# Attention's tails moved behind the second outputs, and batch 2's transposes gathered into two runs

## The chip, the cores and the metric

The kernel runs on one core of one Trainium2 chip. The metric is the device time of one execution in microseconds; the median of three runs before the change is 314.04 us (313.4 to 314.63). PE is the matrix engine TensorE, ACT is ScalarE, DVE is VectorE, POOL is GpSimd, SP is SyncE, whose queue only issues DMAs.

## What is computed

The reference runs a causal attention with a decay, whose result is the input of a two-layer perceptron (cut to what matters):

```python
batch, n_heads, seq, head_dim = (8, 8, 576, 64)
scores = scale * np.matmul(q, k.transpose(0, 1, 3, 2))
cum = np.cumsum(np.maximum(s, 0.0), axis=-1)
bias = -(cum[:, :, :, None] - cum[:, :, None, :])
scores = np.where(causal, -1000000000.0, scores + np.minimum(bias, 0.0))
attn = softmax(scores)
x = matmul(attn, v).transpose(0, 2, 1, 3).reshape(B * S, H * D)    # 4608 x 512
h = x @ w_in                                                       # 512 x 2048
g = 0.5 * h * (1.0 + erf(h * inv_sqrt2))
return g @ w_out                                                   # 2048 x 512
```

## The kernel before

**Tiling.** The eight batches of attention give 8 x 576 = 4608 tokens, which the perceptron takes as nine chunks of 512. Chunk c needs the tokens of batches up to c alone, so batch c + 1 is computed inside chunk c. The work has no scheduler: each engine runs its instructions in the order in which the code issues them, so a line that is moved moves in every queue that it issues to.

**Attention of one batch.** q and k are transposed (for batches 0 to 2 on PE, `tr_mm`, L395, in 64 x 64 tiles, 36 matmuls for one of q and k of four heads; later by DMA). `sc_mm` (L434) makes scores, ACT takes their exponentials into `P` (L440), DVE masks them (`mask`, L448 and L453). `av_mm` (L463) multiplies by the values with tiles of 128 rows by 32 columns, four side by side: the denominators `av_d` (weights from `wb`) and the outputs `av_o` (weights from `vv`), for the first 512 rows of two halves of the heads (qd 0 and 1). `av_out` takes the reciprocals on ACT (L478, L479) and writes the product into `xT` on DVE (L503). The last 64 rows of a batch are its **tails**: `av_tails` runs 48 small matmuls into `av_t` (`tails_pe`), two ACT instructions and one DVE product, L524 (`tails_out`). Batch b's tails are first needed by chunk b + 1.

**The perceptron.** `l1_item(c, f2)` is one **pair**: two of the 16 columns of first-layer tiles, 4 + 4 matmuls of 128x512 into one pair of PSUM banks (`h_ps`, L550), and one Gelu on ACT (L558; the last pair's in two halves, L561). The second layer of chunk 0 runs in `l2_item` (L576). From chunk 1 on it is seven products of halves in place of eight (`prod`, L764, 16 matmuls of 128x256 each, results `o_al`, `o_be`, `o_ga`), between which the next batch's scores and outputs stand.

**Banks.** PSUM is held as five slots: x, y and z of two banks each, `M[0]` and `M[1]` of one each. `order[c]` says in which order chunk c uses x, y and z; pair f2 takes the slot f2 modulo 3. A slot is free once its last reader has finished.

**Around the change.** In chunks 0 and 1 the first two pairs are issued as their first two k-tiles, then the tails of batch c (into `M[0]`), then the other two k-tiles (L910 to L914). In chunks 1 to 6 the tails of batch c + 1 stand between product 4 and product 3 (L1046), into the slot y that the batch's first outputs used. In chunk 1, batch 2's four transposes (q and k of two halves) follow pairs 2, 3, 4 and 5 one by one, each into `M[0]` and `M[1]` with two DVE copies (L404). Behind pair 2 ACT runs `squares_v(1)` (L237, two instructions over the values of batch 1, for a check), after which POOL loads the k of batch 3 into the same buffer; behind pair 5 it runs `squares_v(2)`.

Of the kernel before, what the change touches and what calls it, by code (L numbers as in the profile page):

```python
# [19 lines left out]
def kernel(  # L20
# [10 lines left out]
    nc = tc.nc  # L31
# [195 lines left out]
    def absmax(b, p):  # L227

        nc.vector.tensor_reduce(  # L229
            amx[:, b * NP + p], qkT[b % 2][:, :, p, :S], axis=AX, op=ALU.max, apply_absolute_value=True  # L230
        )
# [174 lines left out]
    def tr_two(b, qd, i, engs):  # L406
        t_ps = [bank(m, [128, FR, 64], bf16, "tr_ps") for m in M]
        tr_mm(b, qd, i, t_ps)
        for pp in range(2):
            copy(  # L410
                engs[pp],
                qkT[b % 2][:, i, 2 * qd + pp, :S].rearrange("d (t r) -> d t r", r=FR),
                t_ps[pp].rearrange("d r t -> d t r"),
            )
# [73 lines left out]
    def av_pe(b, qd, den, two):  # L488

        oo = bank(two, [128, 2, 512], fp32, "av_o")  # L490
        o = [oo[:, t] for t in range(2)]
        av_mm(b, qd, den, None, MAIN)
        for t in range(2):
            av_mm(b, qd, o[t], t, MAIN)
        return o
# [12 lines left out]
    def av_main(b, qd, one, two):  # L508
        den = bank(one, [128, 512], fp32, "av_d")
        o = av_pe(b, qd, den, two)  # L510
        av_out(b, qd, den, o)
# [18 lines left out]
    def av_tails(b, slot):  # L530
        tails_out(b, tails_pe(b, slot))
# [364 lines left out]
    mask(0, 3, nc.vector)  # L896
    av_main(0, 0, M[0], Y)
    av_main(0, 1, M[1], Z)

    for c in range(NCH):  # L900
        nb = c + 1
        if nb >= B:
            l1_seven(c)
            if c < B:
                order[c + 1] = order[c]
            sums_a(c, (1, 2), HF // 2, HF)
            l2_seven(c)
            continue
        if c < 2:
            l1_item(c, 0, 0, KO - 2)  # L910
            l1_item(c, 1, 0, KO - 2)
            av_tails(c, M[0])
            l1_item(c, 0, KO - 2)
            l1_item(c, 1, KO - 2)  # L914
        else:
            l1_item(c, 0, 0, KO - 2)
            l1_item(c, 0, KO - 2)
            l1_item(c, 1)
        if 1 < c:
            transpose_tiles(nb)  # L920
            if nb + 1 < B:
                behind_g(qkT[nb % 2][0:1, 1, NP - 1, S - 1 : S])
                for n in "qk":
                    load_qk(nb + 1, n)
        for p in range(NP) if c == 0 else (0, 1) if c == 1 else (0, 1, 2):
            absmax(c, p)
        for f2 in range(2, FT // 2):
            l1_item(c, f2)
            if c == 1 and 2 <= f2 < 6:
                tr_two(2, f2 // 2 - 1, f2 % 2, both)  # L930
            if c == 1 and f2 == 2:
                squares_v(1)
                load_qk(3, "k")
            if c == 1 and 3 <= f2 < 5:
                scale_v(2, STS[f2 - 3 : f2 - 2], nc.vector)
            if c == 1 and f2 == 5:
                sums_a(c, (1, 2, 3), 0, HF // 2)
                scale_v(2, STS[2:4], nc.vector)
                squares_v(2)
            if c > 1 and f2 == 3:  # L940
                scale_v(nb, [(0, 4), (4, 5)], nc.vector)
                sums_a(c, (1, 2, 3), 0, HF // 2)
                absmax(c, 3)
                if c == B - 2:
                    sums_u((1, 2))
                    absmax(nb, 0)
            if c > 1 and f2 == 4:
                squares_v(nb)
                if nb + 1 < B:
                    behind(2, raws[nb + 1, "k"][0:1, ST - 2, 0, :])  # L950
                    load_v(nb + 1, [nc.sync])
        if c == 0:
            squares_v(0)
            sums_b((1, 2, 3, 4), 0, 4)
            exp_set()
            x, y, z = order[0]
            l2_item(c, 0, 0, 8)
            l2_item(c, 1, 0, 8)
            tr_one(1, 0, 0, nc.vector, z)
            tr_one(1, 0, 1, nc.scalar, x)  # L960
            l2_item(c, 2, 0, 8, y)
            sc_mm(1, 0, (z, x))
            l2_item(c, 3, 0, 8, y)
            sc_mm(1, 1, (z, x))
            mask(1, 0, nc.vector)
            sums_b((1, 2, 3), 4, 8)
            behind(1, w_out_r[0:1, FT - 5, 0:D])
            load_v(1, [nc.sync])
            l2_item(c, 0, 8, 12)
            l2_item(c, 1, 8, 12)  # L970
            tr_one(1, 1, 0, nc.vector, z)
            tr_one(1, 1, 1, nc.scalar, x)
            mask(1, 1, nc.vector)
            sums_b((4,), 4, 8)
            behind_v(1, 1)
            for qd in range(2):
                for n in "qk":
                    load_front(2, n, qd)
            l2_item(c, 2, 8, 12)
            l2_item(c, 3, 8, 12)  # L980
            sc_mm(1, 2, (z, x))
            l2_item(c, 0, 12, eng=nc.scalar)
            sc_mm(1, 3, (z, x))
            mask(1, 2, nc.vector)
            scale_v(1, STS, nc.vector)
            l2_item(c, 1, 12, eng=nc.scalar)
            l2_item(c, 2, 12, eng=nc.scalar)
            mask(1, 3, nc.vector)
            av_main(1, 0, M[0], z)
            l2_item(c, 3, 12)  # L990
            av_main(1, 1, M[1], x)
            order[1] = (y, z, x)
            load_v(2, [nc.sync])
            load_qk(3, "q")
        else:
            exp_set()
            sums_a(c, (1, 2), HF // 2, HF)

            x, y, z = order[c]
            order[nb] = (z, x, y)  # L1000
            add = nc.vector.tensor_tensor
            al_t = bank(M[0], [128, 2, 256], fp32, "o_al")
            al = [al_t[:, u] for u in range(2)]
            kept = [keep_sb(i, n) for i, n in enumerate(("q0", "k0", "q1"))]
            oa = [two_sb() for _ in range(2)]

            prod(c, 1, al, start=True)
            sc_mm(nb, 0, (z, x))
            sc_mm(nb, 2, (y,))
            copy(nc.vector, kept[0], al_t)  # L1010
            if c == 1:
                scale_v(2, STS[4:5], nc.vector)
                load_v(3, [nc.sync])
            be = bank(M[1], [128, 2, 256], fp32, "o_be")
            prod(c, 2, [be[:, u] for u in range(2)], start=True)
            prod(c, 6, al, 0, 6)
            mask(nb, 0, nc.vector)
            add(oa[0][:, :, N1], be, kept[0], op=ALU.add)
            sc_mm(nb, 2, (z,), 1)
            sc_mm(nb, 1, (x, y))  # L1020
            mask(nb, 2, nc.vector)
            prod(c, 6, al, 6)
            copy(nc.vector, kept[1], al_t)
            mask(nb, 1, nc.vector)
            sc_mm(nb, 3, (z, x))
            sums_a(c, (3, 4), HF // 2, HF)
            sums_a(c, (4,), 0, HF // 2)
            ga_t = bank(M[1], [128, 2, 256], fp32, "o_ga")
            ga = [ga_t[:, u] for u in range(2)]
            prod(c, 5, ga, start=True)  # L1030
            mask(nb, 3, nc.vector)
            if nb + 1 < B:
                behind_g(P_of[nb, 3][0:1, 1, PW - 1 : PW])
                cast_qk(nb + 1)
            den = bank(z, [128, 2, 512], fp32, "av_d")
            o = av_pe(nb, 0, den[:, 0], y)
            av_out(nb, 0, den[:, 0], o)
            prod(c, 7, al)
            copy(nc.scalar, kept[2], al_t)
            o = av_pe(nb, 1, den[:, 1], x)  # L1040
            add(oa[1][:, :, N2], ga_t, kept[2], op=ALU.add)
            av_out(nb, 1, den[:, 1], o)
            prod(c, 4, al)
            if c == B - 2:
                sums_x(c + 1, nc.vector)
            av_tails(nb, y)  # L1046
            copy(nc.scalar, oa[1][:, :, N1], al_t)
            if c == B - 2:
                nc.scalar.preload_act_table_set("gelu_and_others")
            store(c, 2, oa[1])  # L1050
            prod(c, 3, ga)
            add(oa[0][:, :, N2], ga_t, kept[1], op=ALU.add)
            store(c, 1, oa[0])
            if c == 1:
                absmax(1, 2)
                absmax(1, 3)
                square(7)
            elif nb < B - 1:
                square(c + 1 if c > 2 else 0)
            if c == 2:  # L1060
                cert_decay()
            if c == B - 2:
                sums_u((3,))
# [158 lines left out]
```

## Time and profile before

| | us |
|---|---|
| median of three runs | 314.04 |
| profiled execution | 314.03 |
| its span, first to last instruction | 312.2 |
| PE busy | 293.0 |
| ACT busy | 246.7 |
| DVE busy | 228.4 |
| POOL busy | 98.8 |

Times within the execution count from the span's start. In the timeline a row is a run of like instructions: start, length, engine, line, operation, output and inputs, shape, count, and in square brackets the idle time of the engine ahead of it with what ended it. Matmuls overlap in the array and their ends are modelled, so a row's length runs past the next row's start; the difference of two starts is the time that a run holds PE's queue. In the rows `128*128`, `128*32` and `64*64` are the tile of the array that a matmul uses. The chain of work lists what led to the last instruction, back from the end, in order of time.

### The profile page before, as it was taken

The page shows a single profiled execution, that of the slowest core. Times are in us where ns is not written, and L with a number is a line of the kernel's source. Part 1 is how long each engine was busy: PE and PEld are TensorE (multiplying, and loading weights), DVE is VectorE, ACT ScalarE, POOL GpSimd, SP SyncE. Part 2 cuts the span into 40 slices and gives each one's busy share as a digit, 9 for nine tenths or more (in the row PEclk, how much of TensorE's full clock was granted, in tenths as well). Part 3 has the DMA queues.
Part 4 walks back from the last instruction along what each step waited for, and adds up shares of the span by engine and source line. Part 5 has one row for each costly group of instructions (what it writes and reads, how often), then busy time and mean ns, then how long its engine had stood idle before and what let it go on. Part 6 is the DMA issues. An engine that isn't in the chain of part 4 may idle for free.

```text
span 312.2 us, 8460 instructions
## 1 busy us (share of the span) xinstructions
PE 293.0 (94%) x3522; PEld 194.8 (62%) x3522; DVE 228.4 (73%) x430; ACT 246.7 (79%) x348; POOL 98.8 (32%) x180
## 2 busy tenths in 40 slices
PE   0689999999999999999999999999999999999991
PEld 0564444545784578547854786477647887887780
DVE  3597337788879777696876597748798889856770
ACT  3687687798968996989788988798879877967830
POOL 6585007104070376228530944095500000000000
PEclk9999999999999999999999999999999999999997
DMA  7999999996616696969597859967891030011013
GB/s 110 200 180 206 206 166 188 270 237 155 132 24 193 120 221 127 256 116 214 116 277 140 186 121 232 208 156 150 171 249 20 2 135 5 0 69 68 2 47 98
DMA packets 77933, 45.07 MB, mean 144 GB/s; under 512 B 63168, under 2 KB 70336, under 8 KB 77888
## 3 DMA queue, kind: packets, MB, share of 16 engines
q1 hardware_dynamic: 67104, 24.93, 35.0%
q0 software_dynamic: 10784, 19.53, 32.1%
q8 instruction: 29, 0.48, 0.7%
q14 instruction: 16, 0.13, 0.2%
HBM read 36.85 MB, written 9.44 MB: 148 GB/s over the span
## 4 chain that ended last, share of the span: by engine, by line
PE 84%; DVE 5%; ACT 5%; DMA 2%; issue 1%; POOL 0%; ACTq 0%; POOLq 0%
PE h_ps L550 32%; PE o_al L764 17%; PE o_ga L764 9%; PE h_ps L667 6%; PE sc_ps L434 5%; PE o_be L764 4%; PE av_o L463 4%; PE av_d L463 2%; DMA fk<-in_k_dram 2%; PE o_ps L576 2%; ACT junk L237 2%; ACT P L440 2%; DVE vv L247 2%; PE av_t L463 1%; PE tr_ps L395 1%
## 5 line engine op out<-in xcount | busy, mean ns | idle before, releaser
L550 PE MATMUL h_ps<-xT,w_in_r 128*128 128x512 f16 x480 | 106.4, 379 | 0.5 <-DVE o_sb L404 0.5
L550 PEld LDWEIGHTS <-w_in_r 128*128 128x128 f16 x480 | 46.3, 98 | 53.9 <-issue 0.8
L440 ACT ACTIVATE P<-sc_ps 128x1024 bf16<-128x1024 f32 x64 | 60.2, 1032 | 3.4 <-PE sc_ps L434 3.3
L558 ACT ACTIVATE gT<-h_ps 128x1024 f16<-128x1024 f32 x49 | 48.3, 1018 | 13.2 <-PE h_ps L550 13.0
L764 PEld LDWEIGHTS <-S 128*128 128x128 f16 x512 | 47.8, 98 | 8.4 <-issue 0.9
L229 DVE TENSOR_REDUCE amx<-qkT 128x2 f32<-128x1152 bf16 x32 | 41.6, 1345 | 0.3 <-DMA qkT<-qk_bf 0.3
L764 PEld LDWEIGHTS <-gT 128*128 128x128 f16 x384 | 36.5, 98 | 7.6 <-issue 2.2
L448 DVE TENSOR_TENSOR P<-P,tri_bf 128x512 bf16<-128x512 bf16 x64 | 25.9, 420 | 11.3 <-ACT P L440 10.7
L754 DVE TENSOR_TENSOR S<-gT 128x1024 f16<-128x1024 f16 (+1 forms) x30 | 21.6, 722 | 14.0 <-ACT gT L561 12.1
L764 PE MATMUL o_al<-T,S 128*128 128x256 f16 x256 | 31.7, 273 | 0.0
L197 POOL DMA_DIRECT2D raw_k<-in_k_dram x25 | 21.1, 850 | 13.8 <-DMA raw_v<-in_v_dram 13.8
L434 PE MATMUL sc_ps<-qkT 64*128 64x256 bf16 (+2 forms) x320 | 22.3, 264 | 3.0 <-DVE qkT L404 1.7
L503 DVE TENSOR_TENSOR xT<-av_o,ln 128x256 f16<-128x256 f32 (+2 forms) x72 | 23.8, 387 | 1.6 <-ACT ln L479 1.2
L247 DVE TENSOR_TENSOR vv<-raw_v,wb 128x512 bf16<-128x512 f32 (+2 forms) x25 | 24.0, 1002 | 0.0
L197 POOL DMA_DIRECT2D raw_q<-in_q_dram x25 | 21.1, 858 | 0.9 <-POOL seen_v L148 0.9
L434 PEld LDWEIGHTS <-qkT 64*128 64x128 bf16 x320 | 13.9, 98 | 12.0 <-issue 6.7
L237 ACT ACTIVATE junk<-raw_v 128x2048 bf16<-128x2048 f32 (+1 forms) x16 | 20.3, 1268 | 0.3
L404 DVE COPY qkT<-tr_ps 128x576 bf16<-128x576 bf16 (+1 forms) x15 | 12.0, 834 | 10.1 <-PE tr_ps L395 10.1
L681 DVE TENSOR_TENSOR k<-h_ps,k 128x512 f32<-128x512 f32 (+1 forms) x12 | 11.3, 956 | 8.1 <-PE h_ps L667 5.5
L479 ACT ACTIVATE ln<-ln,lnb 128x256 f32<-128x256 f32 x32 | 16.3, 509 | 1.0
L148 POOL CAST seen_v<-qkT 1x1 f32<-1x1 bf16 x4 | 1.2, 304 | 48.5 <-DMA qkT<-qk_bf 48.5
L463 PE MATMUL av_o<-P,vv 128*32 128x256 bf16 (+1 forms) x512 | 16.5, 270 | 0.0
(132 smaller groups left out, 439.2 us busy)
## 6 DMA issues: line engine op xcount, KB each, us to landing
raw_v<-in_v_dram SPq DMA_DIRECT2D x32, 256.0 KB, 4.8
out_dram<-o_sb SPq DMA_DIRECT2D x14, 512.0 KB, 4.0
raw_q<-in_q_dram POOLq DMA_DIRECT2D x20, 256.0 KB, 4.6
raw_k<-in_k_dram POOLq DMA_DIRECT2D x20, 256.0 KB, 6.6
w_out_r<-in_moe_w_out_dram POOLq DMA_DIRECT2D x4, 512.0 KB, 13.0
out_dram<-o_sb SPq DMA_DIRECT2D x7, 256.0 KB, 7.2
fq<-in_q_dram POOLq DMA_DIRECT2D x6, 288.0 KB, 7.0
fk<-in_k_dram POOLq DMA_DIRECT2D x6, 288.0 KB, 8.1
```

The costliest lines, as they stand in the source:

```text
L197: nc.gpsimd.dma_start(out=t[:n_st, st], in_=src)
L229: nc.vector.tensor_reduce(amx[:, b * NP + p], qkT[b % 2][:, :, p, :S], axis=AX, op=ALU.max, apply_absolute_value=True)
L237: nc.scalar.activation(n[:n_st, : (st1 - st0) * H * D], t[:n_st, st0:st1].rearrange("p s h d -> p (s h d)"), func=AF.Square, accum_out=amv ...
L247: eng.tensor_tensor(vb[:n_st, st0:st1, h0:h1, :], t[:n_st, st0:st1, h0:h1, :], wb[:n_st, st0:st1, b * H + h0 : b * H + h1] .unsqueeze(3).t ...
L434: nc.tensor.matmul(s_ps[:, e, off : off + n], lhsT=qkT[b % 2][e * 64 : e * 64 + 64, 1, p, jt * 128 : jt * 128 + 128], rhs=qkT[b % 2][e * 6 ...
L440: nc.scalar.activation(P[:, :, UO[u] : UO[u] + UW[u]], s_ps[:, :, : UW[u]], func=AF.Exp, scale=scale)
L448: eng.tensor_tensor(d, d, tri_bf.unsqueeze(1).unsqueeze(1).to_broadcast([128, 2, 2, 128]), op=MULT)
L463: nc.tensor.matmul(o[g * 32 : g * 32 + 32, lo : lo + n], lhsT=(wb[:, jt, b * H + 2 * g + qd : b * H + 2 * g + qd + 1].to_broadcast([128, 3 ...
L503: nc.vector.tensor_tensor(xT[:, 2 * qd + t, x0 : x0 + hi - lo], o[t][:, c * 256 + lo : c * 256 + hi], ln[:, c * 256 + lo : c * 256 + hi], ...
L550: nc.tensor.matmul(h_ps[:, i, :], lhsT=w_in_r[:, ko, ft * 128 : (ft + 1) * 128], rhs=xT[:, ko, c * NB % XW : c * NB % XW + NB], start=(ko ...
L558: nc.scalar.activation(gT_of[c][:, f2 * 2 : f2 * 2 + 2, :], h_ps, func=AF.Gelu)
L764: nc.tensor.matmul(o[u], lhsT=lhs[:, f, u * 128 : u * 128 + 128], rhs=rhs[:, f], start=start and j == 0 and (by_sub or u == 0), stop=j == ...
```

## The change

Three edits. The tails of batches 0 and 1 follow the batch's last `av_main` directly, ahead of the chunk's first layer. The tails of batches 2 to 7 are split: their matmuls (`tails_pe`) follow `av_pe` of the second half of heads, their ACT and DVE part (`tails_out`) stays behind product 4. In chunk 1 batch 2's transposes follow pairs 2 and 4, q and k of a half together: q into `M[0]` and `M[1]`, k into the pair of banks `s0` or `s1`, which is copied by one DVE instruction (`tr_one`). The pairs of chunk 1 behind them no longer go round three slots, and `squares_v(1)` with the K load stands behind pair 3.

```diff
     av_main(0, 1, M[1], Z)
+    av_tails(0, M[0])
...
             l1_item(c, 0, 0, KO - 2)
             l1_item(c, 1, 0, KO - 2)
-            av_tails(c, M[0])
             l1_item(c, 0, KO - 2)
             l1_item(c, 1, KO - 2)
...
+        s0, s1, s2 = order[c]
         for f2 in range(2, FT // 2):
-            l1_item(c, f2)
-            if c == 1 and 2 <= f2 < 6:
-                tr_two(2, f2 // 2 - 1, f2 % 2, both)
-            if c == 1 and f2 == 2:
+            l1_item(c, f2, slot=(s2, s1, s2, s0, s2, s0)[f2 - 2] if c == 1 else None)
+            if c == 1 and f2 in (2, 4):
+                tr_two(2, f2 // 2 - 1, 0, both)
+                tr_one(2, f2 // 2 - 1, 1, nc.vector, (s0, s1)[f2 // 2 - 1])
+            if c == 1 and f2 == 3:
                 squares_v(1)
                 load_qk(3, "k")
...
             av_main(1, 1, M[1], x)
+            av_tails(1, M[0])
...
-            x, y, z = order[c]
+            x, y, z = order[c] if c > 1 else (s2, s0, s1)
...
             o = av_pe(nb, 1, den[:, 1], x)
+            o_t = tails_pe(nb, y)
             add(oa[1][:, :, N2], ga_t, kept[2], op=ALU.add)
             av_out(nb, 1, den[:, 1], o)
             prod(c, 4, al)
             if c == B - 2:
                 sums_x(c + 1, nc.vector)
-            av_tails(nb, y)
+            tails_out(nb, o_t)
```

PE's queue in chunk 1, around the tails of batch 2 (`o_al<-T_111,gT` is product 4, `o_ga<-w_out_r,S_113` product 3). Before, the end of product 4, and then the end of the tails:

```order
L764 MATMUL o_al<-T_111,gT 128x256
L463 LDWEIGHTS wb
L463 MATMUL av_t<-P,wb 32x64
...
L463 LDWEIGHTS vv_116
L463 MATMUL av_t<-P,vv_116 32x64
L764 LDWEIGHTS S_113
L764 MATMUL o_ga<-w_out_r,S_113 128x256
```

Now, the end of the second outputs, and then the end of the tails:

```order
L463 MATMUL av_o<-P,vv_116 32x128
L463 LDWEIGHTS wb
L463 MATMUL av_t<-P,wb 32x64
...
L463 LDWEIGHTS vv_116
L463 MATMUL av_t<-P,vv_116 32x64
L764 LDWEIGHTS gT
L764 MATMUL o_al<-T_111,gT 128x256
```

The tails moved from behind product 4 to ahead of it; product 3 follows product 4 directly.

ACT's queue in the first layer of chunk 1 (`gT` are the Gelus, `raw_v` the squares):

```order
 L479 ACTIVATE lnt<-lnt,lnb 128x128
 L558 ACT_TABLE_LOAD
-L558 ACTIVATE gT<-h_ps 128x1024 x3
-L237 ACTIVATE junk,amv<-raw_v 128x2048
-L237 ACTIVATE junk,amv<-raw_v 64x512
-L558 ACTIVATE gT<-h_ps 128x1024 x3
+L558 ACTIVATE gT<-h_ps 128x1024 x4
+L237 ACTIVATE junk,amv<-raw_v 128x2048
+L237 ACTIVATE junk,amv<-raw_v 64x512
+L558 ACTIVATE gT<-h_ps 128x1024 x2
 L237 ACTIVATE junk,amv<-raw_v 128x2048
 L237 ACTIVATE junk,amv<-raw_v 64x512
```

The first squares stand behind four Gelus in place of three, and two Gelus in place of three lie between the squares.

DVE's queue at the same place (`tr_ps` are the transposes, `raw_v,wb` the values of batch 2 being weighted):

```order
 L229 TENSOR_REDUCE amx<-qkT_119 128x2 x2
-L404 COPY qkT_118<-tr_ps 128x576 x4
+L404 COPY qkT_118<-tr_ps 128x576 x2
+L404 COPY qkT_118<-tr_ps 128x2x576
 L247 TENSOR_TENSOR vv_116<-raw_v,wb 128x512
 L404 COPY qkT_118<-tr_ps 128x576 x2
+L404 COPY qkT_118<-tr_ps 128x2x576
 L247 TENSOR_TENSOR vv_116<-raw_v,wb 128x512
-L404 COPY qkT_118<-tr_ps 128x576 x2
```

Eight copies have become six, of which two are of twice the size, and the second weighting of values stands behind all of them.

## The prediction

> **What bounds the kernel now.** I read the page first, then the waits, then the chain of work that ended last, and last the timeline of the three places that the change touches. The page's first part:
>
> ```profile
> PE 293.0 (94%) x3522; PEld 194.8 (62%) x3522; DVE 228.4 (73%) x430; ACT 246.7 (79%) x348; POOL 98.8 (32%) x180
> ```
>
> TensorE (PE) is busy 94% of the span, so what shortens its own queue should count, unless something else ends last at that place. The waits between 58 and 98 us, over all engines, have two rows for a matmul:
>
> ```profile
> PE h_ps L550 <- DVE o_sb L404: 0.5, 1, 0.5
> PE sc_ps L434 <- ACT P L440: 0.3, 1, 0.3
> ```
>
> So in chunk 1 PE stands twice: once for a copy by VectorE (DVE), once for the exponentials of ScalarE (ACT). The chain shows which stretches are bound by which engine (start, length, what):
>
> ```profile
> 59.40 1.89 PE h_ps L550 x8
> 61.28 0.49 PE av_t L463 x48
> ...
> 78.94 2.86 ACT P L440 x3
> 81.84 0.40 PE sc_ps L434 x6
> ...
> 92.16 0.48 PE av_t L463 x48
> ...
> 252.21 0.48 PE av_t L463 x48
> ```
>
> PE leads from 59.40, ACT leads up to 81.84, and from there the tails `av_t` stand in a chain of PE work alone, up to those of the last batch at 252.21. A shorter PE queue therefore counts in full behind 81.84, and ahead of it only as far as ACT starts its exponentials earlier.
>
> **Part 1: the tails of batches 2 to 7.** These are PE and DVE rows of the timeline of chunk 1's second layer (start, length, engine, line):
>
> ```profile
> 87.66 1.54 DVE L503 TENSOR_TENSOR xT<-av_o,ln 128x256 f16<-128x256 f32 x6
> 88.97 0.57 PE L463 MATMUL av_d<-P,wb 128*32 128x256 bf16 x16
> 89.37 0.94 PE L463 MATMUL av_o<-P,vv 128*32 128x256 bf16 x32
> 90.24 1.92 PE L764 MATMUL o_al<-T,gT 128*128 128x256 f16 x16
> 92.09 0.30 PE L463 MATMUL av_t<-P,wb 128*32 128x64 bf16 x16
> 92.21 0.43 PE L463 MATMUL av_t<-P,vv 128*32 128x64 bf16 x32
> 92.58 1.92 PE L764 MATMUL o_ga<-w_out_r,S 128*128 128x256 f16 x16
> 94.33 2.97 PE L550 MATMUL h_ps<-xT,w_in_r 128*128 128x512 f16 x13
> ```
>
> I count from start to start. Sixteen 128x256 matmuls take 94.33 - 92.58 = 1.75 when the next run is also 128*128, and 92.09 - 90.24 = 1.85 when the next run is in tiles of 128*32: going into the narrow tiles costs 0.10. Coming out: the 32 tails take 92.58 - 92.21 = 0.37, and by the pace of the 16 ahead (0.12 to 0.13) they would take 0.25, so 0.12; the 32 `av_o` take 90.24 - 89.37 = 0.87 where 16 `av_d` of the same widths take 0.40, so 0.07. I take 0.10. Today PE goes out behind `av_o`, in ahead of the tails, and out behind them. With the tails right behind `av_o` one way out and one way in are gone: **0.20 per batch**, from 0.17 to 0.22 by the rows. The new seam, `av_o` to `av_t`, is in no trace. Its nearest row is `av_d` to `av_o`, where 16 matmuls take 0.40 and half of the next 32 would take about 0.40 too, so nothing; its upper end is a whole way in, 0.10. I take nothing, since tile shape and row kind are the same.
>
> The tails now come 1.85 earlier and need bank y, where the first outputs lie until DVE has made xT of them. That ends at 87.66 + 1.54 = 89.20; the second `av_o` run ends about 90.24 - 0.10 = 90.14. Slack 0.9, so no wait; products 4 and 3 are queued behind it. ACT and DVE keep their order at this place; product 4 behind the tails needs ACT's copy of `o_al`, which has 0.5 more time than before. Six batches, all on PE's chain: 6 x 0.20 = **1.20**.
>
> **Part 2: the tails of batch 0.** There the tails stand between eight and 56 first-layer matmuls:
>
> ```profile
> 22.41 1.90 PE L550 MATMUL h_ps<-xT,w_in_r 128*128 128x512 f16 x8
> 22.58 1.57 DVE L503 TENSOR_TENSOR xT<-av_o,ln 128x256 f16<-128x256 f32 x4 [0.22 <-ACT ln L479]
> 24.24 0.30 PE L463 MATMUL av_t<-P,wb 128*32 128x64 bf16 x16
> ```
>
> The same way out and in go: **0.20**. The first eight matmuls start 0.37 later, when their operands are long there, and the next eight, which need the xT that DVE ends at 24.15, would start at about 22.3 + 0.37 + 0.10 + 1.73 = 24.5. PE is the last one there up to the Gelu of the last pair, and ACT's stretch behind it is released by that Gelu, so the gain goes on to batch 1.
>
> **Part 3: batch 1 and chunk 1.** Today the tails cost PE 0.10 going in and 0.49 to the next run. They move ahead of the first layer, into the 0.5 in which PE waits for the `o_sb` copy: 0.37 of tails and 0.10 of way out just fit, the more so as that wait is counted from a modelled end and a run may start 0.07 ahead of one (89.37 + 0.94 = 90.31 against 90.24). The first layer starts at 59.40 as before, and PE gains 0.10 + 0.49 = 0.59 at once. Then the transposes:
>
> ```profile
> 40.37 0.48 PE L395 MATMUL tr_ps<-ident_bf,fq 64*64 64x64 bf16 x36
> 41.11 1.90 PE L576 MATMUL o_ps<-w_out_r,gT 128*128 128x512 f16 x8
> ...
> 47.99 0.48 PE L395 MATMUL tr_ps<-ident_bf,fq 64*64 64x64 bf16 x36
> 48.81 1.90 PE L576 MATMUL o_ps<-w_out_r,gT 128*128 128x512 f16 x8
> ...
> 65.67 1.90 PE L550 MATMUL h_ps<-xT,w_in_r 128*128 128x512 f16 x8
> 67.50 0.48 PE L395 MATMUL tr_ps<-ident_bf,fk 64*64 64x64 bf16 x36
> 67.91 1.90 PE L550 MATMUL h_ps<-xT,w_in_r 128*128 128x512 f16 x8
> 70.15 1.90 PE L550 MATMUL h_ps<-xT,w_in_r 128*128 128x512 f16 x8
> 72.39 3.63 PE L550 MATMUL h_ps<-xT,w_in_r 128*128 128x512 f16 x16
> 75.85 1.91 PE L764 MATMUL o_al<-w_out_r,gT 128*128 128x256 f16 x16
> ```
>
> A 128x512 matmul is (75.85 - 72.39) / 16 = 0.216, a pair's eight 1.73. With transposes behind them the eight take 67.50 - 65.67 = 1.83, so 0.10 in; a run of 36 takes 0.41. The two 72-runs of batch 1 take 41.11 - 40.37 = 0.74 and 48.81 - 47.99 = 0.82. With the way in 0.84 to 0.92 against 2 x 0.51 = 1.02. I take 0.84, since the run at 40.37 stands behind 16 long matmuls, and the first new one behind 24.
>
> But ACT ends this stretch, and its queue is reordered: `squares_v(1)` goes behind the fourth Gelu. Its rows:
>
> ```profile
> 63.87 2.85 ACT L558 ACTIVATE gT<-h_ps 128x1024 f16<-128x1024 f32 x3
> 66.60 1.92 ACT L237 ACTIVATE junk<-raw_v 128x2048 bf16<-128x2048 f32 x1
> 69.28 1.91 ACT L558 ACTIVATE gT<-h_ps 128x1024 f16<-128x1024 f32 x2
> 72.09 1.02 ACT L558 ACTIVATE gT<-h_ps 128x1024 f16<-128x1024 f32 x1 [0.90 <-PE h_ps L550]
> 73.01 1.90 ACT L237 ACTIVATE junk<-raw_v 128x2048 bf16<-128x2048 f32 x1
> 75.66 1.00 ACT L558 ACTIVATE gT<-h_ps 128x1024 f16<-128x1024 f32 x1
> 76.57 1.06 ACT L561 ACTIVATE gT<-h_ps 128x512 f16<-128x512 f32 x2
> ```
>
> A Gelu holds ACT (66.60 - 63.87) / 3 = 0.91, the two squares 2.68 and 2.65, the last Gelus and the table load behind them 78.94 - 76.57 = 2.37. Gelu of pair 5 starts 0.21 behind its matmuls (70.15 + 1.73 = 71.88, 72.09). In the changed kernel pair 3's matmuls end at 59.40 + 24 x 0.216 + 0.84 + 1.73 = 67.15, its Gelu starts at 67.36, and from there ACT has no gap: 0.91 + 2.68 + 0.91 + 0.91 + 2.65 + 0.91 + 2.37 = 11.34. The exponentials start at 78.70 where they start at 78.94 now: **0.24**, or 0.16 with the slower 72-run. The two bank pairs add a wait: pair 6 needs the Gelu of pair 4, now behind the squares; this ends at 67.36 + 0.91 + 2.68 + 1.02 = 72.0, and PE would be ready at 67.15 + 1.73 + 0.84 + 1.73 = 71.5. Behind that matmul on PE's queue are pairs 6 and 7 and product 1; the wait of 0.5 is hidden, since pair 6's Gelu can't start before ACT ends its second squares (71.9 + 0.91 + 2.65 = 75.4) anyway. If ACT were faster there, PE would show up to 0.5 of it. Pair 5's bank holds transposes until DVE has copied them, and the K load of batch 3, in POOL's queue, waits for the later squares (they free its buffer):
>
> ```profile
> 70.27 1.42 DVE L404 COPY qkT<-tr_ps 128x576 bf16<-128x576 bf16 x2 [0.22 <-PE tr_ps L395]
> 69.91 4.22 POOL L197 DMA_DIRECT2D raw_k<-in_k_dram  x5 [13.85 <-DMA raw_v<-in_v_dram]
> 91.17 3.27 POOL L207 CAST qk_bf<-raw_k 128x512 bf16<-128x512 f32 x8
> ```
>
> Two copies take 1.42, the third is as large as both: with the transposes from 59.40 + 24 x 0.216 + 0.10 = 64.7 all three end at about 68, and pair 5 starts at 67.15 + 1.73 + 0.84 = 69.7. The squares that the K load waits for end 1.7 later (67.36 + 0.91 against 66.60), so it goes out at about 71.6 in place of 69.91; its reader starts at 91.17. Neither is late.
>
> **Sum.** 1.20 + 0.20 + 0.24 = 1.64, by the ends of the rows 1.35 to 1.78. The profiled execution took 314.03 (span 312.2 and 1.8 around it, which stays), the median is 314.04, so the two need no correction. 314.03 - 1.64 = **312.4**.
>
> **The rivals.**
> - *The new seam is not free.* If `av_o` to `av_t` costs a way in, seven batches (batch 1's is hidden) gain 0.10 each: 0.70 + 0.24, 313.1. For it: no row shows this seam. Against it: `av_d` to `av_o` shows none. 0.09.
> - *Chunk 1 gives nothing*, since ACT starts later than I count: 312.6. 0.08.
> - *ACT does not bind chunk 1*, and PE's 0.59 and 2 x 0.10 to 0.18 come through: up to 2.3, 311.7. Against it: ACT has no gap from 73.01 to 81.84. 0.10.
> - *Slower: bank y.* DVE frees it 0.9 ahead of the tails; from there each further microsecond holds PE's whole queue in all six chunks, and from 1.2 the change as a whole loses. With y free 1.5 us later than now, each loses 0.6 and gains 0.2: 6 x 0.4 less 0.44 is 2.0 more than now, 316.0. For it: DVE works without a gap ahead of these products. Against it: their order on DVE stays and they end at 89.20 whatever PE does behind. 0.06.
> - *Slower: the granted clock.* If PE's clock halved behind each 72-run, the eight matmuls behind it would take 1.73 more; the first run delays pair 3 and with it ACT's whole stretch, the second pair 5, which has 0.2 of slack there (its Gelu could start at 71.7, ACT is free at 71.9): 3.2 more less 1.64, 315.6. Against it: behind the 72-run at 47.99 eight matmuls show 1.90, as they do elsewhere. 0.03.
>
> The Trainium skill ("TensorE: Matmul & The Clock Gate", Part 4) says that transposes do not count as PE activity for that gate, which speaks against lengthening their runs. Its Part 1 puts the window at 3.4 us, and by that estimate a run of 0.8 would not close it; by Part 4 alone the time would be the last rival's; the trace's 72-run goes against that.
>
> **How the numbers follow.** The forecast case has 0.64. A measurement of this kernel can tell about 0.5%, or 1.57, from no change; the forecast lies 0.07 beyond that border, so 0.46 of it counts as faster and 0.18 as same. With the 0.10 of the third rival: faster 0.56; same 0.18 + 0.09 + 0.08 = 0.35; slower 0.09. The range goes from the third rival, 311.7, to 313.4, a little above the first, and leaves out the slower cases and the scatter of a median.
>
> **What would show it.** Right: 16 `o_al` ahead of `o_ga` take 1.75 in six chunks, no `av_t` row waits for DVE xT, the step from chunk to chunk is 31.8 in place of 32.0, and the exponentials of batch 2 start about 0.4 earlier (0.2 of it batch 0's), with a wait of PE for a Gelu of about 0.5 near 72. Wrong: a gap between `av_o` and `av_t`, a gap of ACT between pair 3's Gelu and the exponentials, or slower matmuls behind a 72-run.

## The result and the profile after

| | before | after |
|---|---|---|
| median, six runs each, us | 314.09 (313.40 to 314.85) | 312.16 (311.56 to 312.71) |
| ratio, with its 95% interval | | 0.9936 (0.9916 to 0.9955) |
| profiled execution, its span | 314.03, 312.2 | 312.71, 310.8 |

The changed kernel is 0.64% faster, between 0.45% and 0.84%: 1.4 to 2.6 us where 1.64 was forecast. The two profiled executions differ by less, 1.3 us. They also differ where no edit reaches: the first transposes were released 0.7 us earlier in the one after (the DMA of `fk` leads the chain for 5.66 in place of 6.37), and its last store ended 0.6 later (7.74 from the last matmul's start to the end of the span, 7.09 before; 6.6 to 7.7 over all profiles of this study). So I compare stages of the program, each from one start of a matmul to another.

The chain of work after the change, at the places where the prediction quoted the one of before (start, length, what; the first layer of chunks 2 to 6 is `h_ps` x64):

```profile
58.70 5.34 PE h_ps L550 x24
...
77.98 2.86 ACT P L440 x3
...
93.35 13.81 PE h_ps L550 x64
...
125.17 13.81 PE h_ps L550 x64
...
220.63 13.81 PE h_ps L550 x64
```

The same view of the kernel before:

```profile
94.50 13.81 PE h_ps L550 x64
...
126.50 13.81 PE h_ps L550 x64
...
222.53 13.81 PE h_ps L550 x64
```

From chunk 2's first layer to chunk 6's it is 127.28 us, 31.82 a chunk, where it was 128.03 and 32.01. Batch 2's tails stand in chunk 1's second layer: from the first `av_o` there to chunk 2's first matmul it is 7.89 where it was 8.08, the sixth saving of 0.19. From chunk 1's first matmul to the first exponentials of batch 2 it is 19.28 where it was 19.54.

| stage, by starts of matmuls, us | before | after | forecast |
|---|---|---|---|
| third `av_d` of batch 0 to first `o_ps` (chunk 0's first layer) | 18.41 | 18.41 | -0.20 |
| first `o_ps` to chunk 1's first matmul | 22.57 | 22.61 | 0 |
| chunk 1's first matmul to the first `av_o` of batch 2 | 26.85 | 26.59 | -0.24 |
| step from chunk to chunk, six times | 32.01 | 31.82 | -0.20 each |

Chunk 1's second layer shows the tails at their new place (PE, DVE; start, length, what):

```profile
86.71 1.54 DVE L503 TENSOR_TENSOR xT<-av_o,ln 128x256 f16<-128x256 f32 x6
88.41 0.94 PE L463 MATMUL av_o<-P,vv 128*32 128x256 bf16 x32
89.18 0.29 PE L463 MATMUL av_t<-P,wb 128*32 128x64 bf16 x16
89.30 0.46 PE L463 MATMUL av_t<-P,vv 128*32 128x64 bf16 x32
89.69 1.92 PE L764 MATMUL o_al<-T,gT 128*128 128x256 f16 x16
91.44 1.91 PE L764 MATMUL o_ga<-w_out_r,S 128*128 128x256 f16 x16
93.19 2.11 PE L550 MATMUL h_ps<-xT,w_in_r 128*128 128x512 f16 x9
```

`av_o` holds PE 89.18 - 88.41 = 0.77, where with a way out behind it it took 0.87. The 48 tails hold it 89.69 - 89.18 = 0.51, where they held it 92.58 - 92.09 = 0.49, so the seam costs 0.02 at most. Product 4 takes 91.44 - 89.69 = 1.75 where it took 1.85: its way in to the tails is gone. DVE frees bank y at 86.71 + 1.54 = 88.25, and the tails start 0.93 later (0.93 to 1.06 over the six batches).

In chunk 1's first layer (PE, then ACT):

```profile
64.28 0.52 PE L395 MATMUL tr_ps<-ident_bf,fk 64*64 64x64 bf16 x36
64.73 3.63 PE L550 MATMUL h_ps<-xT,w_in_r 128*128 128x512 f16 x16
68.29 0.48 PE L395 MATMUL tr_ps<-ident_bf,fq 64*64 64x64 bf16 x36
...
69.05 1.90 PE L550 MATMUL h_ps<-xT,w_in_r 128*128 128x512 f16 x8
71.30 3.61 PE L550 MATMUL h_ps<-xT,w_in_r 128*128 128x512 f16 x16 [0.34 <-ACT gT L558]
```

```profile
66.67 1.02 ACT L558 ACTIVATE gT<-h_ps 128x1024 f16<-128x1024 f32 x1 [1.56 <-PE h_ps L550]
67.59 1.90 ACT L237 ACTIVATE junk<-raw_v 128x2048 bf16<-128x2048 f32 x1
...
70.25 1.91 ACT L558 ACTIVATE gT<-h_ps 128x1024 f16<-128x1024 f32 x2
72.06 1.90 ACT L237 ACTIVATE junk<-raw_v 128x2048 bf16<-128x2048 f32 x1
...
74.71 1.00 ACT L558 ACTIVATE gT<-h_ps 128x1024 f16<-128x1024 f32 x1
75.61 1.06 ACT L561 ACTIVATE gT<-h_ps 128x512 f16<-128x512 f32 x2
76.69 1.28 ACT L863 ACT_TABLE_LOAD   x1
77.98 1.94 ACT L440 ACTIVATE P<-sc_ps 128x1024 bf16<-128x1024 f32 x2
```

The Gelu of pair 3 starts 66.67 - 58.70 = 7.97 behind the first matmul (forecast 67.36 - 59.40 = 7.96), the exponentials 19.28 (forecast 19.30), and between them no row of ACT has an idle time ahead of it. POOL's load of K goes out at 70.88, 12.18 behind the first matmul. PE's wait for a Gelu at pair 6 is there, 0.34 in place of 0.5. Behind the run of 72 transposes 16 matmuls take 68.29 - 64.73 = 3.56, which is 16 x 0.216 and a way in: full pace.

### The profile page after: what moved, and what is told of

It is laid out like the page before. It is cut to its first block, busy times and chain, and to the rows that moved or that the text cites. A ratio compares the mean times of both kernels' runs of the same rounds, so it can differ in the third digit from the quotient of the medians.

```text
span 310.8 us, 8463 instructions
## 1 busy us (share of the span) xinstructions
PE 291.5 (94%) x3522; PEld 196.3 (63%) x3522; DVE 227.4 (73%) x428; ACT 247.1 (80%) x348; POOL 98.3 (32%) x180
## 4 chain that ended last, share of the span: by engine, by line
PE 84%; ACT 6%; DVE 4%; DMA 2%; issue 2%; POOL 0%; ACTq 0%; POOLq 0%
PE h_ps L550 31%; PE o_al L764 17%; PE o_ga L764 9%; PE h_ps L667 6%; PE sc_ps L434 5%; PE o_be L764 4%; PE av_o L463 4%; ACT junk L237 3%; PE av_d L463 2%; DMA fk<-in_k_dram 2%; PE o_ps L576 2%; ACT P L440 2%; DVE vv L247 2%; PE tr_ps L395 1%; PE av_t L463 1%
## 5 line engine op out<-in xcount | busy, mean ns | idle before, releaser
L558 ACT ACTIVATE gT<-h_ps 128x1024 f16<-128x1024 f32 x49 | 49.0, 1018 | 18.6 <-PE h_ps L550 18.5
L197 POOL DMA_DIRECT2D raw_k<-in_k_dram x25 | 21.0, 849 | 15.5 <-ACT junk L237 15.5
L434 PEld LDWEIGHTS <-qkT 64*128 64x128 bf16 x320 | 13.8, 98 | 12.2 <-issue 6.9
L463 PEld LDWEIGHTS <-vv 128*32 128x32 bf16 x768 | 16.3, 100 | 0.6 <-DVE vv L247 0.2
```

The costliest lines, as they stand in the source:

```text
L197: nc.gpsimd.dma_start(out=t[:n_st, st], in_=src)
L434: nc.tensor.matmul(s_ps[:, e, off : off + n], lhsT=qkT[b % 2][e * 64 : e * 64 + 64, 1, p, jt * 128 : jt * 128 + 128], rhs=qkT[b % 2][e * 6 ...
L463: nc.tensor.matmul(o[g * 32 : g * 32 + 32, lo : lo + n], lhsT=(wb[:, jt, b * H + 2 * g + qd : b * H + 2 * g + qd + 1].to_broadcast([128, 3 ...
L558: nc.scalar.activation(gT_of[c][:, f2 * 2 : f2 * 2 + 2, :], h_ps, func=AF.Gelu)
```

## The experiments

Every ratio is to the kernel before on the same chip, with its 95% interval; `before`'s medians there were 313.86 to 314.04.

### One part of the change at a time

**e1_late**: the kernel before with part 1 alone.

```diff
             o = av_pe(nb, 1, den[:, 1], x)
+            o_t = tails_pe(nb, y)
...
-            av_tails(nb, y)
+            tails_out(nb, o_t)
```

> The kernel before with part 1 alone: only the tails of batches 2 to 7 follow the second outputs. My theory (a way out of the narrow tiles and a way in saved, the seam free): the step from chunk to chunk is 31.82 in place of 32.01, six times 0.19, so 1.15 us faster than before, 312.9; everything up to chunk 1's first layer as before. Rival (the gain depends on the other edits, for example on ACT's earlier stretch in chunk 1): a step between 31.82 and 32.01.

Measured: 312.81 us, ratio 0.9961 (0.9947 to 0.9975), a step of 31.82. Chunk 1's stage stays at 26.85. Part 1 needs no other edit, and gives 1.14 by stages, 0.8 to 1.7 by the interval.

**e2_batch0**: the kernel before with batch 0's tails alone at their new place.

```diff
     av_main(0, 1, M[1], Z)
+    av_tails(0, M[0])
...
-            av_tails(c, M[0])
+            if c == 1:
+                av_tails(1, M[0])
```

> The kernel before with only batch 0's tails moved ahead of the first layer. The stretch from the first av_d matmul to the first second-layer matmul (o_ps) took 18.41 us before and 18.41 in the changed kernel. Theory A (the saving of 0.20 is there, but the matmuls of batch 0 went from half pace to full pace 0.2 later against PE's own work in that one execution): the stretch lies between 18.2 and 18.4, by where the pace changes. Theory B (the move saves nothing here, since the four column tiles are out of step at this seam): 18.41 again, wherever the pace changes. Both: no more than 0.2 of the whole time, the step from chunk to chunk 32.01.

Measured: 313.76 us, ratio 0.9999 (0.9986 to 1.0012). The stretch (counted from the third `av_d`; two matmuls stand ahead of a wait) took 18.68, longer than either theory gave: the pace changed later still in this execution (the section on batch 0 has the moments). Nothing follows from this run alone; all runs together are taken below.

**e3_chunk1**: the kernel before with part 3 alone (batch 1's tails, batch 2's transposes, the banks and the squares, as in the change).

> The kernel before with part 3 alone: batch 1's tails ahead of chunk 1's first layer, batch 2's transposes in two runs, the pairs on other banks, the first squares behind pair 3. My theory (ACT binds the stretch from the Gelu of pair 3 to the exponentials): from the first matmul of chunk 1's first layer to the first av_o of batch 2 26.59 us in place of 26.85, so 0.25 faster in all, 313.8. Rival (PE's savings of 0.59 and 2 x 0.1 to 0.18 come through): 26.0 to 26.2, 313.3.

Measured: 313.39 us, ratio 0.9981 (0.9966 to 0.9996); chunk 1's stage 26.59 where it was 26.85, the rest as before. That is my number for the stage. The median of 313.39 is nearer to the rival's 313.3 than to my 313.8, and its interval has room for both; the stage decides, and in it PE's own savings don't come through.

### The price of a change of tile: e6_split

```diff
-            o_t = tails_pe(nb, y)
+            o_t = tails_pe(nb, y, (None,))
...
             prod(c, 4, al)
...
+            tails_pe(nb, y, (0, 1), o_t)
             tails_out(nb, o_t)
```

> The changed kernel with the tails of batches 2 to 7 in two pieces: the 16 denominators behind the second outputs, the 32 others behind product 4, so that PE goes into and out of the narrow tiles once more per batch; their ACT and DVE part stands where it is. My theory (a way in and a way out cost 0.10 each): the step from chunk to chunk 32.02 in place of 31.82, 1.2 us slower than the changed kernel, 313.4, like the kernel before. Rival (the gain comes from the earlier start of the tails, not from the number of changes of tile): a step between 31.82 and 31.9.

Measured: 312.90 us, ratio 0.9963 (0.9945 to 0.9980), a step of 31.99. PE's rows around product 4 of chunk 2's batch:

```profile
120.63 0.94 PE L463 MATMUL av_o<-P,vv 128*32 128x256 bf16 x32
121.40 0.29 PE L463 MATMUL av_t<-P,wb 128*32 128x64 bf16 x16
121.62 1.92 PE L765 MATMUL o_al<-T,gT 128*128 128x256 f16 x16
123.47 0.42 PE L463 MATMUL av_t<-P,vv 128*32 128x64 bf16 x32
123.82 1.92 PE L765 MATMUL o_ga<-w_out_r,S 128*128 128x256 f16 x16
```

Nothing waits there. Product 4 takes 123.47 - 121.62 = 1.85 again, with its way in, and the 16 `av_t` take 0.22 where they take 0.12 without a way out. One more way out and in costs 0.17 per batch, and the gain of part 1 is all but gone, though the tails' first piece starts as early as in the changed kernel. By the steps, the number of changes of tile sets the gain, not when the tails start. The time is 0.5 below the 313.4 that was expected, and its interval (312.1 to 313.2) leaves that out: the medians show more gain than the stages here too, and no stage names where.

### The rival with bank y: e7_late_y, e8_late_y_before

One line more, in the changed kernel and in the one before:

```diff
+            absmax(nb, 2)
             av_out(nb, 0, den[:, 0], o)
```

> The changed kernel with one more reduction on DVE (1.26 us, a maximum that it takes again) ahead of the first products of each of batches 2 to 7, so that the bank pair y comes free 1.26 later. It tries the slower rival of the prediction. If that rival's point is right (DVE frees y 0.93 to 1.06 ahead of the tails): PE waits 0.2 to 0.4 for DVE's xT ahead of the tails in each of six chunks, the step is 32.0 to 32.2, and the time 313.4 to 314.1. If the tails have more room than I count: a step of 31.82 and 312.2.

> The kernel before with the same additional reduction. There the tails stand behind product 4, 2.9 us behind the end of DVE's first products. My theory: no wait for y, the step stays 32.01 and the time 314.0; the same microsecond of DVE costs the changed kernel 1.5 and this one nothing. Rival (DVE's time is short there by itself): the step grows here as well.

Measured: e7 314.03 us, ratio 0.9997 (0.9977 to 1.0016), steps of 32.06 to 32.19; e8 313.68 us, ratio 0.9989 (0.9969 to 1.0008), a step of 32.01. The tails in e7:

```profile
88.82 0.94 PE L463 MATMUL av_o<-P,vv 128*32 128x256 bf16 x32
89.97 0.30 PE L463 MATMUL av_t<-P,wb 128*32 128x64 bf16 x16 [0.21 <-DVE xT L503]
```

From `av_o` to the tails it is 1.15 in place of 0.77: the whole PE queue stands 0.38 for bank y here, and a chunk takes 0.28 more in the mean. The same microsecond of DVE costs the kernel before nothing. The slower rival is a true mechanism, with the point that the prediction gave it (DVE 0.9 ahead of the tails): 1.26 more of DVE took the whole gain away (6 x 0.28 = 1.7).

### Who binds chunk 1: e4_sq_pair2, e5_sq_early, e11_early_load

**e4_sq_pair2**: the first squares back behind pair 2.

```diff
-            if c == 1 and f2 == 3:
+            if c == 1 and f2 == 2:
                 squares_v(1)
```

> The changed kernel with the first squares (and the load of K behind them) back behind pair 2, where the kernel before has them, and nothing else. Theory (ACT stands 1.56 us for matmuls ahead of the Gelu of pair 3 in the changed kernel, and the squares fit there, but the second squares then wait for the Gelu of pair 5): from the first matmul of chunk 1 to the first av_o of batch 2 26.4 in place of 26.59, and no wait of PE for a Gelu. Rival (it is the place of the first squares that lets chunk 1 gain): 26.85 as before the change.

Measured, one run: 312.77 us; the stage 26.65, neither number. PE's wait for a Gelu at pair 6 is gone, as expected, but a run of 36 transposes took 0.66 here where it takes 0.45, and the Gelu of pair 5, from which ACT's chain runs, started 12.49 behind the first matmul, as in the changed kernel (12.45). Without these 0.21 it would be my 26.4; one run does not show it. The rival's 26.85 is out.

**e5_sq_early**: both squares one pair earlier, pair 7 on the second bank pair.

```diff
-            l1_item(..., slot=(s2, s1, s2, s0, s2, s0)[f2 - 2] if c == 1 else None)
+            l1_item(..., slot=(s2, s1, s2, s0, s2, s1)[f2 - 2] if c == 1 else None)
...
-            if c == 1 and f2 == 3:
+            if c == 1 and f2 == 2:
                 squares_v(1)
                 load_qk(3, "k")
+            if c == 1 and f2 == 4:
+                squares_v(2)
...
-                squares_v(2)
...
-            x, y, z = order[c] if c > 1 else (s2, s0, s1)
+            x, y, z = order[c] if c > 1 else (s2, s1, s0)
```

> The changed kernel with the two squares of chunk 1 each moved one pair ahead (behind pair 2 and pair 4), and pair 7 on the second bank pair. My theory (ACT binds there; it stands 2.55 us for matmuls ahead of the Gelu of pair 3, which the first squares can fill): the exponentials start about 1.1 earlier than in the changed kernel (76.8 to 77.0 by its clock in place of 77.98), PE's waits for a Gelu (0.3) and for P (0.4) go, and the time is 0.5 to 0.7 less than the changed kernel's: 311.5. Rival (ACT doesn't bind, PE does): the exponentials start as now, the time is the changed kernel's within 0.1.

Measured: 311.81 us, ratio 0.9921 (0.9903 to 0.9939), the stage 26.19: 0.40 less than in the changed kernel, not 0.5 to 0.7. ACT's rows say what I had overlooked:

```profile
70.78 1.91 ACT L237 ACTIVATE junk<-raw_v 128x2048 bf16<-128x2048 f32 x1 [1.18 <-DMA raw_v<-in_v_dram]
...
77.63 7.44 ACT L440 ACTIVATE P<-sc_ps 128x1024 bf16<-128x1024 f32 x8
```

The second squares now stand for the load of batch 2's values, and so the exponentials start at 77.63, not 76.8 to 77.0, and PE's wait of 0.4 for P stays.

**e11_early_load**: e5 with that load ahead of the last store of chunk 0 on SP's queue.

```diff
             av_main(1, 0, M[0], z)
+            load_v(2, [nc.sync])
             l2_item(c, 3, 12)
             av_main(1, 1, M[1], x)
             av_tails(1, M[0])
             order[1] = (y, z, x)
-            load_v(2, [nc.sync])
```

> e5_sq_early with the load of batch 2's values put ahead of the last store of chunk 0 on SP's queue, since the second squares stood 1.18 us for that load in e5_sq_early (until 70.78). My theory: the load lands about 2 us earlier, the second squares start at 69.5, the exponentials at 76.7 to 77.0 by that run's clock in place of 77.63, PE's wait of 0.4 for P goes, 0.2 to 0.4 less time than e5_sq_early: 311.5. Rival (the load takes as much longer as it goes out earlier, since the DMA engines are busy from 56 to 64): the exponentials where they are, 311.8.

Measured: **311.06 us**, ratio 0.9896 (0.9879 to 0.9914), the stage 25.72: 0.47 less than in e5_sq_early, where 0.2 to 0.4 was expected; PE's wait for P is gone. Its ACT rows, and behind them its chain of work:

```profile
69.85 1.91 ACT L237 ACTIVATE junk<-raw_v 128x2048 bf16<-128x2048 f32 x1 [0.19 <-DMA raw_v<-in_v_dram]
...
77.00 7.64 ACT L440 ACTIVATE P<-sc_ps 128x1024 bf16<-128x1024 f32 x8
```

```profile
58.80 5.34 PE h_ps L550 x24
...
69.28 5.29 PE h_ps L550 x24
74.56 1.75 PE o_al L764 x16
76.31 0.77 PE sc_ps L434 x14
77.08 1.85 PE o_be L764 x16
```

No ACT work is in the chain from 58.80 up to the exponentials at 79.95. That bears out part 3's reason: as long as ACT led, PE's savings in chunk 1 gave 0.26; with the same PE work and ACT's squares earlier the stage gives 1.13 against the kernel before. By the ratios this version is faster than the kernel before and than the changed one (0.9916 to 0.9955).

### Batch 0: e9_warm, e10_warm_before, e12_filled

Why did part 2 give nothing? The rows of the changed kernel's batch 0:

```profile
19.89 0.87 PE L463 MATMUL av_d<-P,wb 128*32 128x256 bf16 x12
20.45 0.43 PE L463 MATMUL av_o<-P,vv 128*32 128x256 bf16 x2
20.52 0.34 PE L463 MATMUL av_d<-P,wb 128*32 128x128 bf16 x2
20.63 1.21 PE L463 MATMUL av_o<-P,vv 128*32 128x256 bf16 x28
21.63 0.22 PE L463 MATMUL av_t<-P,wb 128*32 128x64 bf16 x4
21.67 0.23 PE L463 MATMUL av_o<-P,vv 128*32 128x128 bf16 x2
```

Two things differ from the later batches. The first `av_o` last 0.42 where those that start from 21.34 on last 0.27: at first four such matmuls take 0.213, and later 0.107, half pace and then full pace. And the four column tiles are out of step (two run `av_t` while the other two still run `av_o`).

The trace's record of the granted clock (the share of full speed that the throttle grants TensorE) tells when: here its first entry is full clock from 21.29 on. Ahead of its first entry the record is empty, and there the page prints 9 all the same. In e4_sq_pair2 and e7_late_y the record starts earlier, and the page shows half clock in its third slice (15.5 to 23.3); before, and e4_sq_pair2:

```profile
PEclk9999999999999999999999999999999999999997
```

```profile
PEclk9959999999999999999999999999999999999997
```

There the clock was full from 13.0 (e7: 12.7) for 3.41, half for the next 6.83, and full from 23.2 (e7: 22.9), within the first layer. In the other kernels that have no additional matmuls ahead of batch 0, this is when full clock began, counted from the third `av_d`, beside the stretch to the first `o_ps`:

| kernel | batch 0's tails | full clock from | stretch |
|---|---|---|---|
| before | old place | 3.29 | 18.41 |
| e1_late | old | 3.06 | 18.35 |
| e3_chunk1 | old | 3.22 | 18.37 |
| e8_late_y_before | old | 4.45 | 18.97 |
| after | new place | 3.59 | 18.41 |
| e5_sq_early | new | 3.72 | 18.61 |
| e2_batch0 | new | 4.16 | 18.68 |
| e11_early_load | new | 4.27 | 18.73 |
| e6_split | new | 4.51 | 18.86 |

The stretch follows that moment, about 0.48 us for each microsecond (from before to e8 0.56 for 1.16, from after to e6 0.45 for 0.92), and the moment differs by 1.4 us between these nine executions. At the same moment the new place is 0.14 faster: e6 against e8 is 0.11 shorter with full clock 0.06 later. So after against before shows 0 because full clock came 0.30 later behind the third `av_d`, which cost what the move had saved; e2's theory A had the right reason, with 0.14 for its 0.20. e5 lies 0.14 off its line: one first-layer matmul at 29.36 starts 0.36 behind the one ahead of it, where they take 0.216. Counted only up to the seventeenth first-layer matmul, all nine lie on their lines within 0.02, and the difference is 0.14 too. (The expectation of e9 has 0.11 for this, since in e6 and e8 every `av_o` is at half pace and the durations alone do not show when it ends.)

To take the pace out I put matmuls ahead of batch 0 in both kernels:

```diff
+    warm = bank(M[0], [128, 512], fp32, "warm")
+    for i in range(10):
+        nc.tensor.matmul(
+            warm, lhsT=qkT[0][:, 1, 0, 0:128], rhs=qkT[0][:, 0, 0, 0:512],
+            start=True, stop=True,
+        )
     av_main(0, 0, M[0], Y)
```

> The changed kernel with ten additional 128x512 matmuls (results not used) on PE ahead of batch 0's outputs, which so far ran at half pace at first (four 128x256 matmuls in 0.213 us, later in 0.107). They delay the start by some 3 us; the question is the stretch from the third av_d matmul to the first o_ps matmul, here against e10_warm_before. Theory A (batch 0's tails save 0.20 once the pace changes outside of the stretch): 0.2 shorter than in e10_warm_before. Theory B (only about 0.1, as e6_split against e8_late_y_before with the pace changing at the same point: 18.86 against 18.97): 0.1 shorter. If the pace depends on how long PE has worked, both stretches fall from 18.4 by 1 or more, or wait for DVE.

> The kernel before with the same ten additional matmuls: the other side of the comparison with e9_warm. Both theories: the stretch falls below 18.4 if the pace is full when it begins; its difference from e9_warm is 0.2 by theory A and 0.1 by theory B.

Measured, one run each: 315.12 and 314.84 us. All of batch 0 ran at full pace in both, but the stretches are 18.34 and 18.31, and neither theory is told apart, since PE stood for something that the profile does not name. In e9 it stood so once more, for 1.34 in chunk 2's tails, so its time is no measure of the change either. A row of e9 and one of e10:

```profile
25.90 0.39 PE L550 MATMUL h_ps<-xT,w_in_r 128*128 128x512 f16 x1 [1.39 <-issue]
```

```profile
25.44 0.20 PE L463 MATMUL av_t<-P,vv 128*32 128x64 bf16 x1 [0.74 <-issue]
```

**e12_filled**: e11 with two such matmuls in each of two waits of PE ahead of batch 0 (ahead of `sc_mm(0, 2)` and of `av_main(0, 0)`).

> e11_early_load with two additional matmuls (results not used) in each of two waits of PE for DVE (0.86 and 0.94 us) ahead of batch 0's outputs. Theory (the half pace lasts until PE has worked for a few microseconds without long gaps): full pace comes some 1 to 4 us earlier, the stretch from the third av_d to the first o_ps falls from 18.73 to 17.5 to 18.2, limited by DVE's products, and the time by 0.5 to 1: 310.3. Rival (the pace changes at a time of its own): no change, 311.1, or 0.2 more where the additional matmuls come late.

Measured: 310.90 us, ratio 0.9910 (0.9888 to 0.9931). That is no more than e11 gives, as far as the intervals tell. But the clock was full from 16.35 on, ahead of the second two:

```profile
14.58 1.46 PE L434 MATMUL sc_ps<-qkT 64*128 64x256 bf16 x14 [0.48 <-PE tr_ps L395]
16.30 0.40 PE L434 MATMUL sc_ps<-qkT 64*128 64x256 bf16 x6 [0.26 <-ACT P L440]
16.64 0.60 PE L905 MATMUL warm<-qkT 128*128 128x512 bf16 x2
...
18.02 0.62 PE L463 MATMUL av_d<-P,wb 128*32 128x256 bf16 x12 [0.44 <-DVE P L448]
```

The stretch fell from e11's 18.73 to 17.76, as the theory has it. That the additional matmuls, the first at 13.49, did this is not shown: in e4 and e7 full clock came at 13.0 and 12.7 without them, and went again. The stretch also began 0.44 later, and chunk 1's stage took 26.00 in place of 25.72, with the second squares standing 0.98 for the load of values again. Whether that belongs to the filling or to the one execution stays open.

## Why the prediction held, step by step

- **Part 1, right.** 6 x 0.20 = 1.20 was forecast, 6 x 0.19 = 1.14 came. The new seam, for which the prediction chose 0 from between 0 and 0.10 with no row of it, is in the trace now, at 0.02: 0.10 gone behind `av_o`, 0.10 gone behind product 4, and 0.02 more in the tails. e6_split prices a way out and in by itself, at 0.17.
- **Part 2, mis-sized.** A gain of 0.20 was forecast; at the same moment of full clock it is 0.14, and the two profiled executions show 0. The step that failed is "The same way out and in go": I carried the price of a seam with the four column tiles in step to one where they are out of step. From the last tail's start to the first matmul of the first layer it is 0.20 there (after, e2, e5 and e11), and 0.13 behind tails in step, in batches 2 to 7 and in batch 0 of the kernel before; this 0.07 is about what is missing. That it comes from the tiles being out of step is argued, not shown (in e9 the tiles are in step, but there the first layer waited for DVE's xT). I also took batch 0's rows for settled, and did not see that its matmuls ran at two paces.
- **Part 3, right to 0.02.** 0.24 forecast, 0.26 came, and for its reason: ACT without a gap from the Gelu of pair 3 on. A 72-run took 0.76 (69.05 - 68.29), with the way in 0.86, inside the 0.84 to 0.92. The wait at pair 6 was 0.34, not 0.5, and the load of K went out 12.2 behind the first matmul, as forecast (71.6 - 59.40).
- **The rivals.** The seam, "chunk 1 gives nothing" and "ACT does not bind" are refuted by e1, by e3, and by e3 with e11. Bank y did not bind; its slack was 0.93 to 1.06, and e7, with 1.26 more of DVE, shows the wait. The clock behind a 72-run stayed full.
- **The sum.** By stages 1.14 + 0.26 + 0 to 0.14 = 1.4 to 1.5, a little under the 1.64; the medians' 1.93 has 1.4 to 2.6 around it, so the two agree, and what the medians show beyond 1.5 is not traced to anything. So far as this rest makes up for what part 2 fell short, the closeness of the median is luck.

## What to carry to other kernels

Count changes of tile shape on TensorE from start to start, and put runs of one shape side by side: here each way out and in was worth 0.14 to 0.19 us, and 1.14 over six batches, with the same matmuls. Before a saving on one engine is booked, find who ends the stretch: in chunk 1 the same PE savings gave 0.26 while ScalarE led, and 1.13 once work that could wait elsewhere was put where ScalarE stood idle and its load was issued in time. When a gain is under one per cent, compare stages of the program, since whole executions of one kernel scattered by as much as the gain (eleven of the kernel before on one chip went from 312.61 to 314.72).

## What the runs showed that was not expected

- TensorE ran at half pace (0.213 for four 128x256 matmuls in narrow tiles, later 0.107) up to 20.7 to 22.1 us in nine traces and up to 22.9 and 23.2 in two more (with full clock from about 13 to 16 in between), at another moment in each execution. In nine of these eleven the page's clock row reads 9 there, since the clock's record is still empty; the durations and the record's first entry show it. The Trainium skill ("TensorE: Matmul & The Clock Gate", Part 1) says that the window that opens the clock runs freely and that the number of slow matmuls varies from run to run; the traces agree, with a change of the clock after 3.41 and another after 6.83 in e4 and e7.
- With PE at full pace from the start of batch 0, it stood 0.74 to 1.39 for nothing that the profile names (e9, e10), and in e9 again for 1.34 in chunk 2.
- The 48 tails, 64 columns each, take 0.36 to 0.38 from the first start to the last in four narrow tiles side by side: 8 ns from start to start.
